# Gathering the attention scores and outputs of a fused attention and gated feed-forward kernel into one block each

## The chip, the cores and the metric

The kernel runs on one core of a Trainium2 chip. The metric is the device time of one execution in microseconds; times are medians of several executions, nearly all of which agree within 0.3%. Almost all executions are with a granted TensorE clock of 0.997 to 1.0 of full speed. The engines are PE (matrix products; PEld is its weight loads), DVE (vector), ACT (activation functions), POOL and SP (here they mostly issue transfers).

## The reference

Four batches of eight heads, 768 positions, head size 64. Each query sees keys less than 16 positions away and one maximum key (with a mean value) for each block of 32 positions; the result is the input of a gated feed-forward layer with a residual:

```python
mask_l = np.abs(pos[:, None] - pos[None, :]) < window          # window 16
scores_all = np.concatenate([scores_l_m, scores_s], axis=-1)   # local, and 24 block keys
a = np.exp(scores_all - max); a = a / (sum + 1e-09)
attn = np.matmul(a, v_all)                                     # v and 24 block means
# ...
g = x @ w_gate; val = x @ w_val                                # x: 3072 x 512, d_ff 1536
ffn_out = gelu(g) * val @ w_out
out = x + sigmoid(x @ w_res) * ffn_out
```

## The kernel before

The work is cut into eight units of 384 positions (half a batch). A unit's feed-forward has a long stage of gate and value products (g and vv, 96 matmuls of 384 columns), then an output stage (f with w_out, r with w_res, 512 columns each). Into the output stage of unit u the attention of unit n = u + 1 is woven, head pair by head pair (four pairs). Its matmuls are small and come in two other forms than the full 128 x 128 ones: a **score** takes 64 rows of the array (one head of the pair in each half), and an **attention output** 64 columns (one tile of 64 queries in each half of the partitions written).

```python
def s_step(u, hp, st, banks=None, tiles=None):      # scores of one pair
    # ... two banks, 384 of 512 columns used in each
    s_mm(u, hp, [x[:, 0:TU] for x in s])            # 12 matmuls
    P = ppool.tile([128, 2, HT, QT], BF16, tag="P", name="P")
    # ... exponential(s) on ACT, one or two instructions
    if u:
        Pf = P.rearrange("p a t q -> p (a t) q")
        nc.vector.tensor_mul(Pf, Pf, maskt.unsqueeze(1).to_broadcast([128, 2 * HT, QT]))

def av_step(u, hp, st, pool=ps_o, tag="ao"):        # outputs of one pair
    # ... 12 matmuls into ao, then
    av_end(hp, st, ao)                              # normalization on DVE

def mid_out(u, st, gvT, nst):                       # output stage of units 1 to 6
    n = u + 1
    other = dict(pool=ps_t, tag="t")
    s_step(n, 0, nst)
    s_step(n, 1, nst, TO2)
    res_step(st, 0)
    res_step(st, 1)
    ffn_step(st, gvT, 0, 0, 4)                      # four of twelve f
    av_step(n, 0, nst)
    xt_dma(0, nst)                                  # transpose for the next unit
    av_step(n, 1, nst, **other)
    xt_dma(1, nst)
    s_step(n, 2, nst)
    s_step(n, 3, nst, MM2)
    # ... (even n: copies on POOL)
    ffn_step(st, gvT, 0, 4, FO)
    ffn_step(st, gvT, 1, 0, 3)
    av_step(n, 2, nst)
    xt_dma(2, nst)
    av_step(n, 3, nst, **other)
    xt_dma(3, nst)
    end_step(u, st, 0)
    ffn_step(st, gvT, 1, 3, FO)
    res_step(st, 2)
    end_step(u, st, 1)
    ffn_step(st, gvT, 2, 0, FO)
    end_step(u, st, 2)
```

Unit 1's attention is woven into unit 0's output stage by another function, `first_out`, which the change leaves as it is.

The softmax here doesn't subtract the row's maximum and nothing guards it: scores larger than these inputs give would overflow.

Of the kernel before, what the change touches and what calls it, by code (L numbers as in the profile page):

```python
# [8 lines left out]
F32 = mybir.dt.float32  # L9
BF16 = mybir.dt.bfloat16  # L10
AF = mybir.ActivationFunctionType
# [4 lines left out]
def kernel(  # L16
# [11 lines left out]
    nc = tc.nc  # L28
    B, H, S, D = q.shape
# [3 lines left out]
    scale = 1.0 / math.sqrt(D)  # L33
# [3 lines left out]
    KO = DM // 128  # L37
    FO = DFF // 128
    QT = 64
    NT = S // QT  # L40
    HT = NT // 2
    TU = S // 2
    NSUB = TU // 128
    NU = 2 * B
    NP = H // 2
# [7 lines left out]
    const = ctx.enter_context(tc.tile_pool(name="const", bufs=1))  # L53
    wpool = ctx.enter_context(tc.tile_pool(name="wpool", bufs=1))
    qk = ctx.enter_context(tc.tile_pool(name="qk", bufs=1))
    work = ctx.enter_context(tc.tile_pool(name="work", bufs=3))
    ppool = ctx.enter_context(tc.tile_pool(name="ppool", bufs=4))
    upool = ctx.enter_context(tc.tile_pool(name="upool", bufs=2))
    ps_mm = ctx.enter_context(tc.tile_pool(name="ps_mm", bufs=4, space=bass.MemoryType.PSUM))
    ps_s = ctx.enter_context(tc.tile_pool(name="ps_s", bufs=1, space=bass.MemoryType.PSUM))  # L60
    ps_o = ctx.enter_context(tc.tile_pool(name="ps_o", bufs=1, space=bass.MemoryType.PSUM))
    ps_t = ctx.enter_context(tc.tile_pool(name="ps_t", bufs=1, space=bass.MemoryType.PSUM))
# [3 lines left out]
    maskt = const.tile([128, QT], BF16, name="maskt")  # L66
# [3 lines left out]
    bias_t = const.tile([128, 1], F32, name="bias_t")  # L70
# [5 lines left out]
    kW = [const.tile([128, NT, NP, 128], BF16, name=f"kW{i}") for i in range(2)]  # L76
    qT = [const.tile([128, NQ, NP, 128], BF16, name=f"qT{i}") for i in range(2)]
    q_nat = const.tile([128, NQ, DM], BF16, name="q_nat")
    vext = [const.tile([128, NT, H, VP], BF16, name=f"vext{i}") for i in range(2)]
    vsum = [const.tile([128, DM], BF16, name=f"vsum{i}") for i in range(2)]  # L80
    vpart = const.tile([128, DM], BF16, name="vpart")
    w_gate = wpool.tile([128, KO, DFF], BF16, name="w_gate")
    w_val = wpool.tile([128, KO, DFF], BF16, name="w_val")
# [55 lines left out]
    with tc.manual_schedule():  # L139
# [159 lines left out]
        def vsum_bc(b, lo, hi, eng):  # L299
            src = vsum[b % 2][96:128, :].rearrange("p (h d) -> p h d", d=D) if b else vblk[96:128, :, 0:D]  # L300
            src = src.unsqueeze(1).to_broadcast([32, hi - lo, H, D])
            eng.tensor_copy(vext[b % 2][96:128, lo:hi, :, 0:D], src)  # L302
# [19 lines left out]
        def s_step(u, hp, st, banks=None, tiles=None):  # L322
            if tiles:
                s, banks = tiles, True
            elif banks:
                s = [p.tile([128, 512], F32, tag=tag, name="s") for p, tag in banks]
            else:
                s2 = ps_s.tile([128, 2, 512], F32, tag="s", name="s")
                s = [s2[:, hh] for hh in range(2)]
            s_mm(u, hp, [x[:, 0:TU] for x in s])  # L330
            P = ppool.tile([128, 2, HT, QT], BF16, tag="P", name="P")
            if banks:
                for hh in range(2):
                    nc.scalar.activation(P[:, hh].rearrange("p t q -> p (t q)"), s[hh][:, 0:TU], AF.Exp,  # L334
                                         scale=scale, bias=bias_t[:])
            else:
                nc.scalar.activation(P.rearrange("p a t q -> p a (t q)"), s2[:, :, 0:TU], AF.Exp,  # L337
                                     scale=scale, bias=bias_t[:])
            if u:
                Pf = P.rearrange("p a t q -> p (a t) q")  # L340
                nc.vector.tensor_mul(Pf, Pf, maskt.unsqueeze(1).to_broadcast([128, 2 * HT, QT]))  # L341
            st["P", hp] = P

        MM2 = ((ps_mm, "mm"),) * 2
        TO2 = ((ps_t, "t"), (ps_o, "ao"))

        def av_step(u, hp, st, pool=ps_o, tag="ao"):
            b, half = u // 2, u % 2
            P = st["P", hp]
            ao = pool.tile([128, NSUB, 2, D + 1], F32, tag=tag, name="ao")  # L350
            for sub in range(NSUB):
                for hh in range(2):
                    for e in range(2):
                        t = 2 * sub + e
                        nc.tensor.matmul(ao[64 * e:64 * e + 64, sub, hh, :], P[:, hh, t, :],  # L355
                                         vext[b % 2][:, half * HT + t, 2 * hp + hh, 0:D + 1],
                                         start=True, stop=True, skip_group_check=True)
            av_end(hp, st, ao)
# [12 lines left out]
        def av_end(hp, st, ao):  # L371
            rz = work.tile([128, NSUB, 2, 1], F32, tag="rz", name="rz")
            nc.vector.reciprocal(rz[:], ao[:, :, :, D:D + 1])  # L373
            xn = st["xn"][:, hp].rearrange("p s (h d) -> p s h d", d=D)
            nc.vector.tensor_mul(xn, ao[:, :, :, 0:D], rz.to_broadcast([128, NSUB, 2, D]))  # L375
# [8 lines left out]
        def xt_dma(ko, st):  # L384
            nc.sync.dma_start_transpose(out=st["xT"][:, ko].rearrange("d (s k) -> d s k", k=128),
                                        in_=st["xn"][:, ko].rearrange("p s d -> p (s d)"))
# [6 lines left out]
        def gv_mm(ps, w, st, fo, kos):  # L393
            for ko in kos:
                nc.tensor.matmul(ps[:, 0:TU], w[:, ko, fo * 128:(fo + 1) * 128], st["xT"][:, ko, :],  # L395
                                 start=(ko == 0), stop=(ko == KO - 1), skip_group_check=True)

        def gv_end(gvT, fo, g, vv):
            ge = work.tile([128, TU], F32, tag="ge", name="ge")
            nc.scalar.activation(ge[:], g[:, 0:TU], AF.Gelu)  # L400
            nc.vector.tensor_mul(gvT[:, fo, :], ge[:], vv[:, 0:TU])  # L401

        def mm_tile(name):
            return ps_mm.tile([128, 512], F32, tag="mm", name=name)
# [13 lines left out]
            gv_end(gvT, 0, g, vv)  # L418

        def fo_last_two(st, gvT):  # L420
            g = [mm_tile("g"), mm_tile("g")]
            for i in range(2):
                gv_mm(g[i], w_gate, st, FO - 2 + i, range(KO))
            for i in range(2):
                vv = mm_tile("vv")
                gv_mm(vv, w_val, st, FO - 2 + i, range(KO))
                gv_end(gvT, FO - 2 + i, g[i], vv)

        def res_step(st, sub):
            ss = slice(sub * 128, (sub + 1) * 128)  # L430
# [7 lines left out]
        def ffn_step(st, gvT, sub, lo, hi):  # L438
            ss = slice(sub * 128, (sub + 1) * 128)
            if lo == 0:  # L440
                st["f", sub] = mm_tile("f")
            for fo in range(lo, hi):
                nc.tensor.matmul(st["f", sub][:], gvT[:, fo, ss], w_out[:, fo, :],  # L443
                                 start=(fo == 0), stop=(fo == FO - 1), skip_group_check=True)
# [32 lines left out]
        mm, t_bank, o_bank = (ps_mm, "mm"), (ps_t, "t"), (ps_o, "ao")  # L477
        keep_warm(12)
        tk, tq, ao = {}, {}, {}
# [11 lines left out]
        st = new_unit()  # L491
        gvT = upool.tile([128, FO, TU], BF16, tag="gvT", name="gvT")
# [66 lines left out]
        s2 = ps_s.tile([128, 2, 512], F32, tag="s", name="gv")  # L559
# [22 lines left out]
        def pool_after(x):  # L582
            nc.gpsimd.tensor_copy(gate2[:], x)
# [31 lines left out]

        def mid_out(u, st, gvT, nst):
            n = u + 1
            other = dict(pool=ps_t, tag="t")
            s_step(n, 0, nst)
            s_step(n, 1, nst, TO2)  # L620
            res_step(st, 0)
            res_step(st, 1)
            ffn_step(st, gvT, 0, 0, 4)
            av_step(n, 0, nst)
            xt_dma(0, nst)
            av_step(n, 1, nst, **other)
            xt_dma(1, nst)
            s_step(n, 2, nst)
            s_step(n, 3, nst, MM2)
            if n % 2 == 0:  # L630
                pool_after(nst["P", 3][0:1, 0, 0, 0:1])
                for i in range(2, 4):
                    vsum_bc(n // 2, 3 * i, 3 * i + 3, nc.gpsimd)
            ffn_step(st, gvT, 0, 4, FO)
            ffn_step(st, gvT, 1, 0, 3)
            av_step(n, 2, nst)
            xt_dma(2, nst)
            av_step(n, 3, nst, **other)
            xt_dma(3, nst)
            end_step(u, st, 0)  # L640
            ffn_step(st, gvT, 1, 3, FO)
            res_step(st, 2)
            end_step(u, st, 1)
            ffn_step(st, gvT, 2, 0, FO)
            end_step(u, st, 2)
# [9 lines left out]
        for u in range(NU):  # L655
            b, half = u // 2, u % 2
# [6 lines left out]
            if u:  # L663
                gvT = upool.tile([128, FO, TU], BF16, tag="gvT", name="gvT")
            for fo in range(0 if u else 2, FO):
# [25 lines left out]
                if half == 1 and nb < B:  # L691
# [11 lines left out]
                    if nb == 1:  # L703
                        if fo == 0:
                            tk = turn_all(k_sb[nb])
                        if fo in (0, 2, 4, 6):
                            hp = (2, 0, 1, 3)[fo // 2]
# [5 lines left out]
            else:  # L713
                nst = new_unit()
                (mid_out if u else first_out)(u, st, gvT, nst)
                st = nst
# [30 lines left out]
```

## Time and profile before

| | before |
|---|---|
| time | 256.43 us (256.35 to 256.56) |
| span of the profile | 254.6 us |
| PE / DVE / ACT busy | 97% / 63% / 51% |
| score matmuls | 384, in the record 9.0 us busy |
| output matmuls in units 1 to 7 | 336, 8.3 us busy |

The two small groups, as the list of PE groups by shape has them (line, shape, count, then busy time and the mean length of one):

```profile
L317 PE MATMUL s<-qT,kW 64*128 64x64 bf16 x384 | 9.0, 191 | 0.0
L355 PE MATMUL ao<-vext,P 128*64 128x65 bf16 x336 | 8.3, 197 | 0.0
```

The second number of a row, 191 ns, is the length of one matmul from start to end, and most of it overlaps its neighbours: 384 x 0.191 would be 73 us, the group holds PE for 9.0. The idle time of both groups is 0.0.

### The profile page before, as it was taken

How to read it: one execution, taken by the hardware profiler on the slowest of the kernel's cores; microseconds unless marked ns; L12 is line 12 of the kernel's file. 1: busy time of each engine (PE TensorE's matmuls, PEld its weight loads, DVE VectorE, ACT ScalarE, POOL GpSimd, SP SyncE). 2: the span in 40 equal slices, each digit the busy share in tenths (PEclk: the TensorE clock that was granted, in tenths of full speed). 3: DMA queues.
4: the chain of work that ended last, by engine and by line, in shares of the span. 5: the costliest groups of instructions: out<-in, count | busy, mean ns of one | idle time of the engine just before them, and what ended most of it. 6: DMA issues, size and time to landing. Idle time of an engine off the chain costs nothing.

```text
span 254.6 us, 5847 instructions
## 1 busy us (share of the span) xinstructions
PE 246.6 (97%) x2303; PEld 139.7 (55%) x2328; DVE 159.4 (63%) x364; ACT 129.6 (51%) x216; POOL 97.3 (38%) x128
## 2 busy tenths in 40 slices
PE   6999999999999999999999999999999999999994
PEld 2676555565545665446544665446545555456544
DVE  6985796397667544858567544958567544854424
ACT  8885468366572337353572337254572337353320
POOL 8895542361506970274406970274404000000000
PEclk9999999999999999999999999999999999999999
DMA  5999999999404999399404999289604400230003
GB/s 80 177 182 197 197 205 207 175 176 222 61 19 121 159 150 150 56 161 171 103 18 120 162 155 153 49 162 170 104 18 115 98 3 0 50 139 0 3 1 124
DMA packets 98107, 29.34 MB, mean 115 GB/s; under 512 B 83224, under 2 KB 94944, under 8 KB 97984
## 3 DMA queue, kind: packets, MB, share of 16 engines
q0 software_dynamic: 68352, 14.76, 66.3%
q1 hardware_dynamic: 29728, 14.21, 25.7%
q8 instruction: 18, 0.29, 0.5%
q14 instruction: 9, 0.07, 0.1%
HBM read 29.36 MB, written 6.29 MB: 140 GB/s over the span
## 4 chain that ended last, share of the span: by engine, by line
PE 93%; DVE 5%; issue 2%; DVEq 0%
PE g L395 25%; PE vv L395 24%; PE f L443 23%; PE r L433 8%; PE s L317 3%; PE ao L355 3%; PE vs L282 1%; PE ao L367 1%; PE tp L220 1%; PE vs L290 1%; DVE ks L237 1%; PE xp L380 1%; DVE o L452 1%; DVE th L449 1%; PE gv L395 1%
## 5 line engine op out<-in xcount | busy, mean ns | idle before, releaser
L401 DVE TENSOR_TENSOR gvT<-ge,vv 128x384 bf16<-128x384 f32 x95 | 52.2, 552 | 48.1 <-PE vv L395 43.9
L400 ACT ACTIVATE ge<-g 128x384 f32<-128x384 f32 x95 | 46.7, 491 | 67.3 <-DVE gvT L401 34.8
L395 PE MATMUL g<-xT,w_gate 128*128 128x384 bf16 x380 | 78.0, 326 | 0.0
L395 PE MATMUL vv<-xT,w_val 128*128 128x384 bf16 x380 | 77.8, 326 | 0.0
L443 PE MATMUL f<-w_out,gvT 128*128 128x512 bf16 x262 | 62.7, 379 | 1.5 <-issue 1.1
L395 PEld LDWEIGHTS <-w_gate 128*128 128x128 bf16 x384 | 37.1, 98 | 26.2 <-issue 1.4
L395 PEld LDWEIGHTS <-w_val 128*128 128x128 bf16 x384 | 37.6, 98 | 24.7
L443 PEld LDWEIGHTS <-gvT 128*128 128x128 bf16 x276 | 25.7, 98 | 29.5
L107 POOL DMA_DIRECT2D vext<-in_v_dram x32 | 24.1, 777 | 15.0 <-DMA w_out<-in_moe_w_out_dram 5.6
L436 ACT ACTIVATE th<-r 128x512 f32<-128x512 f32 x24 | 13.5, 607 | 27.6 <-PE r L433 27.6
L449 DVE SCALAR_TENSOR_TENSOR th<-th,f 128x512 f32<-128x512 f32 (+2 forms) x26 | 16.6, 640 | 14.4 <-PE f L443 14.4
L341 DVE TENSOR_TENSOR P<-P,maskt 128x768 bf16<-128x768 bf16 x28 | 16.2, 580 | 11.0 <-ACT P L337 6.1
L433 PE MATMUL r<-w_res,xT 128*128 128x512 bf16 x88 | 22.7, 380 | 0.4
L302 POOL COPY vext<-vsum 32x1536 bf16<-32x1536 bf16 x12 | 17.2, 1464 | 13.0 <-DMA vsum<-vpart 12.9
L452 DVE SCALAR_TENSOR_TENSOR o<-th,xn 128x512 f32<-128x512 f32 (+2 forms) x26 | 18.2, 701 | 0.9
L375 DVE TENSOR_TENSOR xn<-ao,rz 128x384 bf16<-128x384 f32 x32 | 17.8, 557 | 1.1
L337 ACT ACTIVATE P<-s,bias_t 128x768 bf16<-128x768 f32 x17 | 15.3, 901 | 4.5 <-PE s L317 4.3
L127 POOL DMA_DIRECT2D q_nat<-in_q_dram x18 | 15.8, 899 | 0.9 <-issue 0.7
L334 ACT ACTIVATE P<-s,bias_t 128x384 bf16<-128x384 f32 x30 | 15.7, 579 | 0.0
L237 DVE TENSOR_REDUCE ks<-kW 128x24 bf16<-128x768 bf16 x16 | 15.1, 943 | 0.0
L433 PEld LDWEIGHTS <-xT 128*128 128x128 bf16 x96 | 8.8, 98 | 9.9
L373 DVE RECIPROCAL rz<-ao 128x6 f32<-128x6 f32 x32 | 6.1, 191 | 10.9 <-PE ao L355 10.0
(90 smaller groups left out, 187.1 us busy)
## 6 DMA issues: line engine op xcount, KB each, us to landing
out_dram<-o SPq DMA_DIRECT2D x23, 256.0 KB, 2.2
vext<-in_v_dram POOLq DMA_DIRECT2D x32, 96.0 KB, 6.4
q_nat<-in_q_dram POOLq DMA_DIRECT2D x18, 128.0 KB, 6.4
w_gate<-in_moe_w_gate_dram POOLq DMA_DIRECT2D x6, 256.0 KB, 8.9
w_val<-in_moe_w_val_dram POOLq DMA_DIRECT2D x6, 256.0 KB, 9.3
w_out<-in_moe_w_out_dram POOLq DMA_DIRECT2D x3, 512.0 KB, 14.4
k_nat<-in_k_dram POOLq DMA_DIRECT2D x16, 96.0 KB, 5.8
vext<-vext SPq DMA_DIRECT2D x6, 144.0 KB, 5.4
```

Source lines behind the costliest of these rows:

```text
L107: nc.gpsimd.dma_start(out=vext[b % 2][0:QT, :, h, 0:D], in_=v[b, h].rearrange("(t p) d -> p t d", p=QT))
L237: nc.vector.tensor_reduce(out=ks.rearrange("d (t n) -> d t n", n=2), in_=kw[:, :, 0:QT].rearrange("d t (n w) -> d t n w", w=BLK), axis=myb ...
L302: eng.tensor_copy(vext[b % 2][96:128, lo:hi, :, 0:D], src)
L341: nc.vector.tensor_mul(Pf, Pf, maskt.unsqueeze(1).to_broadcast([128, 2 * HT, QT]))
L375: nc.vector.tensor_mul(xn, ao[:, :, :, 0:D], rz.to_broadcast([128, NSUB, 2, D]))
L395: nc.tensor.matmul(ps[:, 0:TU], w[:, ko, fo * 128:(fo + 1) * 128], st["xT"][:, ko, :], start=(ko == 0), stop=(ko == KO - 1), skip_group_ch ...
L400: nc.scalar.activation(ge[:], g[:, 0:TU], AF.Gelu)
L401: nc.vector.tensor_mul(gvT[:, fo, :], ge[:], vv[:, 0:TU])
L433: nc.tensor.matmul(r[:], st["xT"][:, ko, ss], w_res[:, ko, :], start=(ko == 0), stop=(ko == KO - 1))
L443: nc.tensor.matmul(st["f", sub][:], gvT[:, fo, ss], w_out[:, fo, :], start=(fo == 0), stop=(fo == FO - 1), skip_group_check=True)
L449: nc.vector.scalar_tensor_tensor(th[:, cs], th[:, cs], 1.0, f[:, 0:n], ALU.add, ALU.mult)
L452: nc.vector.scalar_tensor_tensor(o.rearrange("p (k d) -> p k d", d=128), th[:, cs].rearrange("p (k d) -> p k d", d=128), 0.5, x, ALU.mult, ...
```

## The change

The intent: all scores of a unit in one place, in six banks filled to 512 columns, and all outputs in another, with the outputs of the last two pairs computed ahead of their normalizations. Cut to its core:

```diff
-    ppool = ctx.enter_context(tc.tile_pool(name="ppool", bufs=4))
+    p_all = const.tile([128, 2, NP * HT, QT], BF16, name="p_all")
+        def s_all(u):
+            for i in range(3):
+                # i == 0: two banks of the large pool, 1: the double bank, 2: ps_t and ps_o
+                for j in range(8):
+                    hp, t = divmod(8 * i + j, HT)
+                    # ... one score matmul for each of two heads
+                # ... exponentials of 512 columns (i == 1: one of 1024), two masks of 512
+        def av_all(u, st):
+            for hp in range(NP):
+                # ... 12 output matmuls into ps_t, ps_o, and the two halves of the double bank
+                if hp != 2:
+                    for i in range(2 if hp == 3 else hp, hp + 1):
+                        av_end(i, st, aos[i])
+                        if u > 1:
+                            xt_dma(i, st)
 ...
         def mid_out(u, st, gvT, nst):
             n = u + 1
-            other = dict(pool=ps_t, tag="t")
-            s_step(n, 0, nst)
-            s_step(n, 1, nst, TO2)
+            s_all(n)
+            # ... (even n: copies on POOL)
             res_step(st, 0)
             res_step(st, 1)
-            ffn_step(st, gvT, 0, 0, 4)
-            av_step(n, 0, nst)
-            # ... pairs 0 and 1, scores 2 and 3, f, pairs 2 and 3
+            ffn_step(st, gvT, 0, 0, FO)
+            av_all(n, nst)
             end_step(u, st, 0)
-            ffn_step(st, gvT, 1, 3, FO)
+            ffn_step(st, gvT, 1, 0, FO)
```

In `fo_last_two` the Gelus of the last two gate products are also written ahead of the value products.

More of the change, by code (lines that the diff above doesn't have):

```diff
@@ L330, in s_step @@
             s_mm(u, hp, [x[:, 0:TU] for x in s])
-            P = ppool.tile([128, 2, HT, QT], BF16, tag="P", name="P")
+            P = p_all[:, :, hp * HT:(hp + 1) * HT]
             if banks:
@@ L339, in s_step @@
             if u:
-                Pf = P.rearrange("p a t q -> p (a t) q")
-                nc.vector.tensor_mul(Pf, Pf, maskt.unsqueeze(1).to_broadcast([128, 2 * HT, QT]))
+                nc.vector.tensor_mul(P, P, maskt.unsqueeze(1).unsqueeze(1).to_broadcast([128, 2, HT, QT]))
             st["P", hp] = P
+        def s_all(u):
+            b, half = u // 2, u % 2
+            kw, qt = kW[b % 2], qT[b % 2]
+            s2 = None
+            for i in range(3):
+                if i == 0:
+                    s = [ps_mm.tile([128, 512], F32, tag="mm", name="s") for _ in range(2)]
+                elif i == 1:
+                    s2 = ps_s.tile([128, 2, 512], F32, tag="s", name="s")
+                    s = [s2[:, hh] for hh in range(2)]
+                else:
+                    s = [p.tile([128, 512], F32, tag=tag, name="s") for p, tag in TO2]
+                for j in range(8):
+                    hp, t = divmod(8 * i + j, HT)
+                    tt = half * HT + t
+                    for hh in range(2):
+                        ps = slice(hh * 64, hh * 64 + 64)
+                        nc.tensor.matmul(s[hh][:, j * QT:(j + 1) * QT], kw[ps, tt, hp, :],
+                                         qt[ps, tt // 2, hp, (tt % 2) * QT:(tt % 2 + 1) * QT],
+                                         start=True, stop=True, skip_group_check=True)
+                js = slice(8 * i, 8 * i + 8)
+                m = maskt.unsqueeze(1).to_broadcast([128, 8, QT])
+                for hh in range(1 if i == 1 else 2):
+                    if i == 1:
+                        nc.scalar.activation(p_all[:, :, js].rearrange("p a j q -> p a (j q)"), s2[:], AF.Exp,
+                                             scale=scale, bias=bias_t[:])
+                    else:
+                        nc.scalar.activation(p_all[:, hh, js].rearrange("p j q -> p (j q)"), s[hh][:], AF.Exp,
+                                             scale=scale, bias=bias_t[:])
+                for hh in range(2):
+                    nc.vector.tensor_mul(p_all[:, hh, js], p_all[:, hh, js], m)
@@ new lines, in av_all @@
+        def av_all(u, st):
+            b, half = u // 2, u % 2
+            aos = []
+            for hp in range(NP):
+                if hp < 2:
+                    pool, tag = TO2[hp]
+                    ao = pool.tile([128, NSUB, 2, D + 1], F32, tag=tag, name="ao")
+                else:
+                    if hp == 2:
+                        s2 = ps_s.tile([128, 2, 512], F32, tag="s", name="ao")
+                    ao = s2[:, hp - 2, 0:NSUB * 2 * (D + 1)].rearrange("p (s h d) -> p s h d", s=NSUB, h=2)
+                for sub in range(NSUB):
+                    for hh in range(2):
+                        for e in range(2):
+                            t = 2 * sub + e
+                            nc.tensor.matmul(ao[64 * e:64 * e + 64, sub, hh, :], p_all[:, hh, hp * HT + t, :],
+                                             vext[b % 2][:, half * HT + t, 2 * hp + hh, 0:D + 1],
+                                             start=True, stop=True, skip_group_check=True)
+                aos.append(ao)
+                if hp != 2:
[3 more added lines that the diff above has]
+                            xt_dma(i, st)
@@ L420, in fo_last_two @@
         def fo_last_two(st, gvT):
-            g = [mm_tile("g"), mm_tile("g")]
+            ge = []
             for i in range(2):
-                gv_mm(g[i], w_gate, st, FO - 2 + i, range(KO))
+                g = mm_tile("g")
+                gv_mm(g, w_gate, st, FO - 2 + i, range(KO))
+                ge.append(work.tile([128, TU], F32, tag="ge", name="ge"))
+                nc.scalar.activation(ge[i][:], g[:, 0:TU], AF.Gelu)
             for i in range(2):
@@ L426, in fo_last_two @@
                 gv_mm(vv, w_val, st, FO - 2 + i, range(KO))
-                gv_end(gvT, FO - 2 + i, g[i], vv)
+                nc.vector.tensor_mul(gvT[:, FO - 2 + i, :], ge[i][:], vv[:, 0:TU])
         def res_step(st, sub):
@@ L617, in mid_out @@
             n = u + 1
-            other = dict(pool=ps_t, tag="t")
-            s_step(n, 0, nst)
-            s_step(n, 1, nst, TO2)
+            s_all(n)
+            if n % 2 == 0:
+                pool_after(p_all[0:1, 1, 4 * HT - 1, 0:1])
+                for i in range(2, 4):
+                    vsum_bc(n // 2, 3 * i, 3 * i + 3, nc.gpsimd)
             res_step(st, 0)
             res_step(st, 1)
-            ffn_step(st, gvT, 0, 0, 4)
-            av_step(n, 0, nst)
-            xt_dma(0, nst)
-            av_step(n, 1, nst, **other)
-            xt_dma(1, nst)
-            s_step(n, 2, nst)
-            s_step(n, 3, nst, MM2)
-            if n % 2 == 0:
-                pool_after(nst["P", 3][0:1, 0, 0, 0:1])
-                for i in range(2, 4):
-                    vsum_bc(n // 2, 3 * i, 3 * i + 3, nc.gpsimd)
-            ffn_step(st, gvT, 0, 4, FO)
-            ffn_step(st, gvT, 1, 0, 3)
-            av_step(n, 2, nst)
-            xt_dma(2, nst)
-            av_step(n, 3, nst, **other)
-            xt_dma(3, nst)
+            ffn_step(st, gvT, 0, 0, FO)
+            av_all(n, nst)
             end_step(u, st, 0)
-            ffn_step(st, gvT, 1, 3, FO)
+            ffn_step(st, gvT, 1, 0, FO)
             res_step(st, 2)
```

## The prediction

> **What bounds the kernel now.** I read the page first (busy shares, then the chain that ended last), then the PE groups by shape, then the timeline of one output stage, then the lists of waits.
>
> ```profile
> PE 246.6 (97%) x2303; PEld 139.7 (55%) x2328; DVE 159.4 (63%) x364; ACT 129.6 (51%) x216; POOL 97.3 (38%) x128
> ...
> PE 93%; DVE 5%; issue 2%; DVEq 0%
> PE g L395 25%; PE vv L395 24%; PE f L443 23%; PE r L433 8%; PE s L317 3%; PE ao L355 3%; PE vs L282 1%; PE ao L367 1%; PE tp L220 1%; PE vs L290 1%; DVE ks L237 1%; PE xp L380 1%; DVE o L452 1%; DVE th L449 1%; PE gv L395 1%
> ```
>
> The matmul engine is the bound: 97% busy, and 93% of the chain that ended last is PE. Of its 254.6 us span the score matmuls (s) hold 3% and the attention outputs (ao, two lines) 4%; the large products that the change doesn't touch hold the rest. So the change can only win in how PE passes between these, or lose by making PE wait. Busy time can't show a pass, since the ends of matmuls are modelled; start times can. Here is the output stage of unit 2 (it computes unit 3's attention), cut to what I use; columns are start, length, engine, line, operation, count, and idle time before with its releaser:
>
> ```profile
> 96.59 1.46 PE L395 MATMUL vv<-xT,w_val 128*128 128x384 bf16 x8
> ...
> 97.30 1.28 ACT L337 ACT_TABLE_LOAD   x1
> 97.51 1.21 DVE L401 TENSOR_TENSOR gvT<-ge,vv 128x384 bf16<-128x384 f32 x2 [1.40 <-PE vv L395]
> 97.98 0.41 PEld L317 LDWEIGHTS <-kW 64*128 64x128 bf16 x24 [0.32 <-issue]
> ...
> 98.44 1.41 PEld L433 LDWEIGHTS <-xT 128*128 128x128 bf16 x8
> ...
> 99.39 1.05 ACT L334 ACTIVATE P<-s,bias_t 128x384 bf16<-128x384 f32 x2
> 99.53 0.56 DVE L341 TENSOR_TENSOR P<-P,maskt 128x768 bf16<-128x768 bf16 x1 [0.81 <-ACT P L337]
> ...
> 100.18 1.03 PE L443 MATMUL f<-w_out,gvT 128*128 128x512 bf16 x4
> ...
> 101.13 0.46 PEld L355 LDWEIGHTS <-P 128*64 128x64 bf16 x24 [0.42 <-DVE P L341]
> 101.63 0.41 PEld L317 LDWEIGHTS <-kW 64*128 64x128 bf16 x24
> 102.09 2.06 PEld L443 LDWEIGHTS <-gvT 128*128 128x128 bf16 x11
> 102.50 5.80 SPq L385 DMA_TRANSPOSE xT<-xn  x4
> ...
> 104.57 0.46 PEld L355 LDWEIGHTS <-P 128*64 128x64 bf16 x24 [0.42 <-DVE P L341]
> 105.07 1.62 PEld L443 LDWEIGHTS <-gvT 128*128 128x128 bf16 x9
> 107.03 1.03 PE L433 MATMUL r<-w_res,xT 128*128 128x512 bf16 x4
> 109.53 0.18 POOL L583 COPY gate<-xT 1x1 bf16<-1x1 bf16 x1 [4.34 <-DMA xT<-xn]
> 110.48 0.65 PE L395 MATMUL g<-xT,w_gate 128*128 128x384 bf16 x3
> ```
>
> The reader should see four blocks of small matmuls (97.98, 101.13, 101.63, 104.57) between runs of full ones. A full 512-column matmul starts every 0.217 us (eight r plus four f from 98.44 to 101.04); 24 scores take 98.44 - 97.98 = 0.46 us, 24 outputs 101.63 - 101.13 = 0.50. From the first score to the next g at 110.48 the stage is 12.50 us: 48 scores 0.92, 48 outputs 1.00, 36 f and 12 r 10.40, together 12.32. Left over is 0.18.
>
> That 0.18 sits ahead of the two blocks of outputs. Four f from 100.18 would free PE at 101.05, the outputs start at 101.13; eleven f from 102.09 would end at 104.48, the outputs start at 104.57. The step from the gate/value products into the scores costs the same: the last vv starts at 97.73, would be followed at 97.89, the first score starts at 97.98. The brackets call the weight load before the outputs a wait for the masks on DVE, but in unit 3's stage the mask ended 0.10 us before the outputs, and the gap after the last f is the same, so it is the switch. Passes from small blocks to full ones, and from outputs to scores, cost nothing visible.
>
> **What the Trainium skill says.** "TensorEngine Tiling (Array Packing)", section Key Properties: changing the tiling mode drains TensorE. The trace agrees in one direction: about 0.09 us on entering a small block from full matmuls, none measurable on leaving. "TensorE: Matmul & The Clock Gate", section Back-to-back issue gap: an isolated warm gap of N/2.4 + 2.5 ns, 216 ns for 512 columns; the trace has 217. "ScalarE: Activation LUTs", section What ACT_TABLE_LOAD costs: 1283 ns for the load of a table; the trace has 1283 for each of the seven loads ahead of the exponentials, which is why no exponential starts before 98.59. "VectorE: DVE Perf Modes", section on the 8-slice pipeline in each mode: packed 16-bit operands give two results a cycle. The trace agrees: a mask over 768 bf16 elements takes 580 ns, a product of 384 f32 elements 552.
>
> **The change, part by part.** It concerns six stages (the attention of units 2 to 7). I count from the stage's first score, T = 0.
>
> *Switches.* Before, PE enters a small block from full matmuls three times (scores, outputs, outputs); after, twice. One entry of 0.09 us less in each of six stages: 0.55 us. No matmul is removed: 48 scores and 48 outputs stay.
>
> *Exponentials.* Before, two of 768 columns and four of 384; after, four of 512 and one of 1024. From 901 and 579 ns, 0.84 ns a column; the 384-column ones start 0.53 us apart and the 768-column one is followed 0.80 us later, so 512 columns take 0.63 and 1024 about 1.02. Sum 4 x 0.63 + 1.02 = 3.55 against 2 x 0.80 + 4 x 0.53 = 3.7: 0.15 less, off the path. They begin when the table is loaded (T = 0.61), end about T = 4.2.
>
> *Masks.* Before, four of 580 ns; after, six of 512 columns, 580 - 256 x 0.52 = 447 ns each: 2.7 against 2.3 us. The last one follows the last exponential, T = 4.75.
>
> *When PE needs them.* Scores T = 0 to 0.92, eight r and twelve f to 0.92 + 20 x 0.217 = 5.26, a switch, outputs from 5.35 to 6.35. The first needs only the masks of the first group; the last pair, at 6.1, needs the mask of T = 4.75. No wait, 1.3 us to spare. The scores' banks are free in time too: the two packed banks in the large pool were the last two gate products', read by the Gelus before the table load at 97.30.
>
> *Normalizations and transposes.* The four now come together. Before, the outputs' start at 101.13 leads to the first transpose's issue at 102.50, 1.37 later; after, T = 6.72. DVE then needs 0.75 us a pair (191 + 557 ns), but the four transposes leave their queue 1.28 us apart (102.50 and 103.78 before), so the issues are 6.72, 8.0, 9.28 and 10.56. Landing takes 2.3 us: the fourth arrives at T = 12.9. The next unit's first three parts start at T = 12.41 and its fourth part is asked for six matmuls of 0.1625 us later, T = 13.38. So 0.5 us to spare, where before it was 109.4 against 111.46, 2.0 us. This is the tightest place.
>
> *Sum.* 256.43 - 0.55 = 255.9. The change of the Gelus ahead of the value products and the buffer of P move no instruction on the path; each pair's P was already held once per unit (four buffers, four pairs).
>
> **The rivals.** (1) *A wait for the last transpose replaces the switch.* For: 0.5 us to spare, while single transposes landed in up to 3.7 us, and the queue would carry four in a row. Against: in the three stages that gate a load on it, the fourth landed 2.3 to 2.5 us after issue. If it came 0.8 late throughout, 0.3 us a stage, 6 x 0.3 = 1.8: 257.7.
> (2) *The query load comes too late.* POOL holds the next queries' load until the fourth transpose has landed, now 1.3 us later (T = 12.9 against 11.55). In units 3 and 5 the transposed queries landed at 125.2 and 182.7, the scores started at 127.04 and about 184.85: slack 1.8 and 2.1. What remains is 0.5 to 0.9; a loss of a microsecond in two stages would give 257 to 258.
> (3) *All P in one tensor ties engines together.* If the build orders accesses by the range that they span, the 1024-column exponential, which spans both heads, waits for the masks of the first group: 0.5 us later, masks end at 5.3, still before T = 6.1. Only if each group waited for all masks of the one before would the masks end near T = 7.2, PE stop for 1 to 2 us a stage, and the time be 262 to 268. The before kernel works in slices of shared tensors throughout and shows no such waits; I give it 3%.
> (4) *The bound moves to DVE or ACT.* DVE is at 8.3 us of this stage's 12.5, ACT at 7.2; 0.4 more and 0.15 less change nothing.
>
> **Range and chances.** Certain is only the one switch per stage; a switch hidden in the passes that I see as free could add as much again (255.3). Against it stand small waits of rivals 1 and 2. I say 255.9 us, 255.1 to 257.6. 2% is 5.1 us: a gain of that is nine times what the switches hold (1%); a loss of that needs rival 3 or a stall of 0.9 us in every stage (4%).
>
> **What would show it.** Right: in the changed profile the outputs of all four pairs start about 5.35 us after the first score, in one block of 48; from first score to next g about 12.4 us; the fourth transpose lands before the fourth part of g asks for it; no new PE wait in the list. Wrong: a gap in g before its fourth part (rival 1), scores late behind a query transpose in two stages (rival 2), exponentials with idle time ahead of them released by masks (rival 3), or a pace of scores other than 0.019 us or of outputs other than 0.021 us in the longer blocks.

## The result, and the profile after

| | before | changed |
|---|---|---|
| time, median | 256.5 us (256.35 to 256.77, 4 runs) | 254.5 us (254.38 to 255.01, 4 runs) |
| ratio | 1 | 0.9925, 95% interval 0.9907 to 0.9942 |
| span of the profile | 254.6 us | 252.9 us |
| first score to next g, unit 2 | 12.50 us | 12.17 us |

Ratios here are the mean time of one kernel's fast runs over that of the other's in the same rounds, so not quite the ratio of the medians. Executions over 1.5% slower than the fastest of the same kernel are left out of the means. The change gained 2.0 us where 0.55 was predicted, and 254.5 lies below the range of 255.1 to 257.6. It is still "within 2%", which had been given 95%.

The page of the changed kernel, its line of PE and its chain:

```profile
PE 248.1 (98%) x2328; PEld 139.5 (55%) x2328; DVE 159.0 (63%) x376; ACT 127.9 (51%) x210; POOL 96.5 (38%) x128
...
PE g L451 25%; PE vv L451 24%; PE f L502 24%; PE r L492 8%; PE ao L390 2%; PE s L360 2%; PE vs L282 1%; PE tp L220 1%; PE ao L423 1%; PE vs L290 1%; PE s L317 1%; PE wp L534 1%; DVE ks L237 1%; DVE o L511 1%; PE xp L436 1%
```

The bound is the same. PE's busy time even rises, from 246.6 to 248.1 us, while the kernel gets faster; the page before had 2303 matmul records and this one 2328, all of them, so here the difference is one of missing records. The chain alone shows no cause. Start times do. The same stage as in the prediction, the changed kernel, PE only (start, length, engine, line, operation, count):

```profile
97.67 0.87 PE L360 MATMUL s<-qT,kW 64*128 64x64 bf16 x48
98.48 1.90 PE L492 MATMUL r<-w_res,xT 128*128 128x512 bf16 x8
100.22 2.75 PE L502 MATMUL f<-w_out,gvT 128*128 128x512 bf16 x12
102.90 0.95 PE L390 MATMUL ao<-vext,p_all 128*64 128x65 bf16 x48
103.78 2.76 PE L502 MATMUL f<-w_out,gvT 128*128 128x512 bf16 x12
106.39 1.03 PE L492 MATMUL r<-w_res,xT 128*128 128x512 bf16 x4
107.25 2.75 PE L502 MATMUL f<-w_out,gvT 128*128 128x512 bf16 x12
109.84 0.65 PE L451 MATMUL g<-xT,w_gate 128*128 128x384 bf16 x3
```

The 48 scores hold PE for 98.48 - 97.67 = 0.81 us. Before, two blocks of 24 took 0.46 each, 0.92 together. The 48 outputs hold it for 103.78 - 102.90 = 0.88 us, before 0.50 and 0.50. So the blocks themselves became 0.23 us shorter though no matmul is missing. With the one entry less (0.09 to 0.10) that is the stage's 0.33 us, and six stages of it are the 2.0 us. All six have it: from first score to next g they take 12.16 to 12.17 us in the changed kernel, and 12.49 to 12.50 before (12.62 in one).

**The theory** that this suggests ("passes"): PE pays about 0.11 us at every pass from one form of matmul to another, in either direction and between the two small forms too. The start times of single matmuls agree. In the changed kernel the scores start in pairs 29 ns apart, the last pair at 98.355 and 98.358, and the first r at 98.480: 0.12 us after, not 0.03. In the kernel before, the last output of the first block starts at 101.510 and the next score at 101.637, 0.13 us after. Counted this way, a stage had seven passes: full to scores, scores to full, full to outputs, outputs to scores, scores to full, full to outputs, outputs to full. The change leaves four. Three times 0.11 is 0.33.

**The rivals:** "packing" (scores are cheaper because they fill six banks and need fewer, larger exponentials), "waits" (something that PE waited for, masks or banks, went away), and "the Gelus" (the small edit in `fo_last_two`).

### The profile page after: what moved, and what is told of

Same layout as the page of the kernel before. It is cut to its first block, busy times and chain, and to the rows that moved or that the text cites. A ratio compares the mean times of both kernels' runs of the same rounds, so it can differ in the third digit from the quotient of the medians.

```text
span 252.9 us, 5881 instructions
## 1 busy us (share of the span) xinstructions
PE 248.1 (98%) x2328; PEld 139.5 (55%) x2328; DVE 159.0 (63%) x376; ACT 127.9 (51%) x210; POOL 96.5 (38%) x128
## 4 chain that ended last, share of the span: by engine, by line
PE 93%; DVE 5%; issue 1%; DVEq 0%
PE g L451 25%; PE vv L451 24%; PE f L502 24%; PE r L492 8%; PE ao L390 2%; PE s L360 2%; PE vs L282 1%; PE tp L220 1%; PE ao L423 1%; PE vs L290 1%; PE s L317 1%; PE wp L534 1%; DVE ks L237 1%; DVE o L511 1%; PE xp L436 1%
## 5 line engine op out<-in xcount | busy, mean ns | idle before, releaser
L456 ACT ACTIVATE ge<-g 128x384 f32<-128x384 f32 x81 | 39.7, 490 | 61.0 <-DVE gvT L457 30.0
L502 PE MATMUL f<-w_out,gvT 128*128 128x512 bf16 x276 | 63.6, 379 | 0.0
L373 DVE TENSOR_TENSOR p_all<-p_all,maskt 128x512 bf16<-128x512 bf16 x36 | 14.2, 423 | 8.3 <-ACT p_all L370 4.5
L511 DVE SCALAR_TENSOR_TENSOR o<-th,xn 128x512 f32<-128x512 f32 (+2 forms) x26 | 16.9, 651 | 0.9
L370 ACT ACTIVATE p_all<-s,bias_t 128x512 bf16<-128x512 f32 x24 | 15.2, 692 | 0.1
```

The lines of the kernel that those rows point to most:

```text
L456: nc.scalar.activation(ge[:], g[:, 0:TU], AF.Gelu)
L502: nc.tensor.matmul(st["f", sub][:], gvT[:, fo, ss], w_out[:, fo, :], start=(fo == 0), stop=(fo == FO - 1), skip_group_check=True)
L511: nc.vector.scalar_tensor_tensor(o.rearrange("p (k d) -> p k d", d=128), th[:, cs].rearrange("p (k d) -> p k d", d=128), 0.5, x, ALU.mult, ...
```

## The experiments

Thirteen runs, all correct. The first four alter the changed kernel without touching packing: three add passes, the fourth only moves them.

**Scores in two blocks.** The first r is put between the 32 scores of the first two groups and the 16 of the third:

```diff
-            s_all(n)
+            s_all(n, (0, 1))
+            res_step(st, 0)
+            s_all(n, (2,))
             # ... (even n: copies on POOL)
-            res_step(st, 0)
             res_step(st, 1)
```

> Changed kernel, with its 48 scores cut in 32 and 16 by the four matmuls of the first r; banks, exponentials and masks as in the changed kernel. Theory 'passes' (every pass of PE from one form of matmul to another costs about 0.11 us, also on leaving a small block, so the change saved three passes of seven in a stage): two passes more, 6 x 0.22 = 1.3 us, so 254.5 + 1.3 = 255.8, and the two blocks of scores last about 0.58 and 0.35 us, 0.12 more in sum than the one block of 0.81. Rival 'packing' (scores are cheaper because they fill six banks, with fewer and larger exponentials): nothing of that is undone, so at most the entry of 0.09 us, 255.0 or less. Rival 'waits' (the gain was waits for masks and banks that went): 254.5 to 255.0.

Measured: 256.1 us (255.79 to 256.23), ratio to the kernel before 0.9977 (0.9965 to 0.999): 0.3 above what passes gave, 1.1 above the most that its rivals allowed. The timeline of unit 2's stage:

```profile
97.95 0.64 PE L360 MATMUL s<-qT,kW 64*128 64x64 bf16 x32
98.52 1.04 PE L492 MATMUL r<-w_res,xT 128*128 128x512 bf16 x4
99.49 0.41 PE L360 MATMUL s<-qT,kW 64*128 64x64 bf16 x16
99.83 1.04 PE L492 MATMUL r<-w_res,xT 128*128 128x512 bf16 x4
...
110.32 0.65 PE L451 MATMUL g<-xT,w_gate 128*128 128x384 bf16 x3
```

Thirty-two scores take 0.57 us, sixteen 0.34. With 0.46 for 24 and 0.81 for 48, the four lengths lie on one line: about 0.105 us for the block and 14.7 ns for each matmul (from 16 and 48: 0.47 / 32 = 0.0147; 0.34 - 16 x 0.0147 = 0.105). The stage is 12.37 us, 0.20 more than the changed kernel's.

**Scores in three blocks.** The same, with both r products between the three groups.

```diff
-            s_all(n)
+            s_all(n, (0,))
+            res_step(st, 0)
+            s_all(n, (1,))
+            res_step(st, 1)
+            s_all(n, (2,))
             # ... (even n: copies on POOL)
-            res_step(st, 0)
-            res_step(st, 1)
```

> Changed kernel, with its 48 scores cut in three blocks of 16 by the two r products. Passes: four passes more per stage, 6 x 0.44 = 2.6 us, 257.1, slower than the kernel before although all packing stays. Packing or waits: two entries of 0.09, at most 6 x 0.18 = 1.1, 255.6.

Measured: 257.0 us (256.89 to 257.35), ratio 1.0019 (1.0006 to 1.0031). All of the change's packing is in this kernel, and it is slower than the kernel before. That rules out packing as the cause, and waits too, for which at most 255.6 had been expected; the list of PE's waits has only that of the first matmul, 1.2 us. The stage is 110.69 - 98.10 = 12.59 us, 0.42 more than the changed kernel's for four passes more.

```profile
98.10 0.41 PE L360 MATMUL s<-qT,kW 64*128 64x64 bf16 x16
98.44 1.04 PE L492 MATMUL r<-w_res,xT 128*128 128x512 bf16 x4
99.41 0.41 PE L360 MATMUL s<-qT,kW 64*128 64x64 bf16 x16
...
110.69 0.65 PE L451 MATMUL g<-xT,w_gate 128*128 128x384 bf16 x3
```

**Outputs in two blocks.** Pairs 0 and 1 after eight f, pairs 2 and 3 after all twelve.

```diff
-            ffn_step(st, gvT, 0, 0, FO)
-            av_all(n, nst)
+            ffn_step(st, gvT, 0, 0, 8)
+            av_all(n, nst, (0, 1), aos)
+            ffn_step(st, gvT, 0, 8, FO)
+            av_all(n, nst, (2, 3), aos)
```

> Changed kernel, with the outputs of pairs 0 and 1 after eight f and those of pairs 2 and 3 after all twelve. Passes: two more per stage, 1.3 us, less up to 0.4 because the first transposes leave 0.9 us earlier and the fourth part of g need not wait (0.18, 0.08 and 0.18 us in the profile of the changed kernel): 255.4 to 255.8. Rivals: 254.1 to 254.6.

Measured: 255.86 us (255.83 to 255.91), ratio 0.9971 (0.9959 to 0.9983). That is 0.06 above what passes gave and 1.3 above the most that the rivals allowed. The two blocks of 24 are back at 0.50 us each. So the outputs' form pays as the scores' does.

**Outputs earlier.** In the first profile of the changed kernel the next unit's fourth part of g started 0.18, 0.08 and 0.18 us late in three stages (units 5, 6 and 7): rival 1 of the prediction, in small. The first of them, with the three parts that precede it:

```profile
166.42 0.65 PE L451 MATMUL g<-xT,w_gate 128*128 128x384 bf16 x3
166.91 0.65 PE L451 MATMUL vv<-xT,w_val 128*128 128x384 bf16 x3
167.57 0.32 PE L451 MATMUL g<-xT,w_gate 128*128 128x384 bf16 x1
```

Six matmuls of 0.1625 us from 166.42 would have led to 167.395. This run moves the outputs ahead by four f, the passes being the same:

```diff
-            ffn_step(st, gvT, 0, 0, FO)
-            av_all(n, nst)
+            ffn_step(st, gvT, 0, 0, 8)
+            av_all(n, nst)
+            ffn_step(st, gvT, 0, 8, FO)
```

> Changed kernel, with all 48 outputs after eight f in place of twelve: same four passes. If the late fourth transpose costs what the profile shows (0.44 us in three stages together), 254.5 - 0.4 = 254.1 and no gap before the fourth part of g; if the last masks (4.5 us after the first score) come too late for the last pair's outputs (at 4.9), a wait of up to 0.3 us a stage takes it back, 254.5 or more.

Measured: 254.46 us (254.28 to 254.56), ratio 0.9915 (0.9902 to 0.9928). The gaps are gone from its profile, but the time is that of the changed kernel. The profiled execution of the changed kernel was the one of 255.01 us; its other three took 254.38 to 254.50. So the late fourth part costs little in most executions. The unaltered changed kernel fits that:

> The changed kernel once more, for a second profile and more times beside the next three: 254.5. If the waits of the fourth part of g (0.44 us in the first profile) come only in some executions, a profile of 252.4 to 252.6 us has none.

Measured: 254.61 us (254.43 to 254.92), ratio 0.9923 (0.9911 to 0.9935). Its profile, of 252.5 us, still has one such gap, of 0.1 us in one stage, so not quite none.

**The cost of a pass, by itself.** Four kernels start from the kernel before and put extra small matmuls between g and vv in nine of the twelve steps of units 2 to 7, 54 places in all. Their operands are zeros and their results are thrown away; only their form differs.

```diff
             gv_mm(g, w_gate, st, fo, range(KO))
+            if extra:
+                x = ps_s.tile([128, 2, 512], F32, tag="s", name="x")
+                for hh in range(2):                       # rows: ps is one half of the partitions
+                    nc.tensor.matmul(x[:, hh, 0:64], warm[ps, 0:128], warm[ps, 128:192], ...)
+                # columns: matmul(x[ps, 0, 0:64], warm[:, 0:64], warm[:, 128:192], ...)
+                # full:    matmul(x[:, hh, 0:64], warm[:, 0:128], warm[:, 128:192], ...)
             vv = mm_tile("vv")
```

> Kernel before, with two extra matmuls of 64 columns between g and v in nine of the twelve steps of units 2 to 7 (54 places), in the form of their neighbours (128 rows, 128 columns of weights), results thrown away. Both theories: no change of form, so only their own time, 0.05 to 0.15 us a place, 2.7 to 8 us: 259 to 264.5.

> The same 54 places, the two extra matmuls in the scores' form (64 rows, one for each half). Passes: entry 0.09, the pair 0.03, leaving 0.12, so 0.24 us a place, 13 us: 269.5. If only entering costs (as the prediction had it): 0.09 + 2 x 0.019 = 0.13, 7 us: 263.5.

> The same 54 places, the two extra matmuls in the outputs' form (64 columns of weights, one for each half of the partitions written). Passes: 0.09 + 0.03 + 0.13 = 0.25 us a place, 13.5 us: 270. If only entering costs: 0.09 + 2 x 0.021, 7 us: 263.5.

> Kernel before, in the 54 places a pair in the scores' form and right after it a pair in the outputs' form. If a pass between the two small forms costs what leaving for full ones costs: entry 0.09, pair, 0.12, pair, 0.13, about 0.37 us a place, 20 us: 276.5. If it is free, as the prediction had it: 0.27, 14.5 us: 271. If it costs as much as leaving and entering: 0.48, 26 us: 282.5.

| extra at each of 54 places | time (median) | more than the median of before | per place |
|---|---|---|---|
| two full matmuls of 64 columns | 259.65 us | 3.17 us | 0.059 us |
| a pair in the scores' form | 269.32 us | 12.84 us | 0.238 us |
| a pair in the outputs' form | 270.18 us | 13.70 us | 0.254 us |
| one pair of each, in a row | 277.83 us | 21.13 us | 0.391 us |

(The kernel before took 256.48 us in the call of the first three and 256.70 in that of the fourth.) A pair in a block takes 0.029 us. Taking that off and dividing by the passes: (0.238 - 0.029) / 2 = 0.105, (0.254 - 0.029) / 2 = 0.113, (0.391 - 2 x 0.029) / 3 = 0.111 us a pass. A pair of each in a row has three passes and not four, and the measured time follows that count: the pass between the two small forms costs as much as one to or from the full form. One place, from the timeline of the kernel with a pair of each:

```profile
90.50 0.81 PE L395 MATMUL g<-xT,w_gate 128*128 128x384 bf16 x4
91.24 0.20 PE L413 MATMUL x<-warm 64*128 64x64 bf16 x2
91.38 0.22 PE L417 MATMUL x<-warm 128*64 128x64 bf16 x2
91.53 0.82 PE L395 MATMUL vv<-xT,w_val 128*128 128x384 bf16 x4
```

Four g from 90.50 would free PE at 91.15. The first pair starts 0.09 later, the second 0.14 after it, vv 0.15 after that. The same place with two full matmuls, which start when the g are through and hand over after 0.06:

```profile
91.69 0.81 PE L395 MATMUL g<-xT,w_gate 128*128 128x384 bf16 x4
92.34 0.22 PE L412 MATMUL x<-warm 128*128 128x64 bf16 x2
92.40 0.81 PE L395 MATMUL vv<-xT,w_val 128*128 128x384 bf16 x4
```

One more rival lies near: a load of weights takes 0.098 us in the profile, about as much as a pass, and a short matmul could be too short to hide it. The two full matmuls load weights just as often, and the whole pair costs 0.059 us. The start times of the loads (PEld) show where the pass lies. Within a run of full matmuls a load starts well ahead of its matmul: in the kernel before, the loads of the four r behind f start at 106.81 and these r at 107.03. Behind the scores, the loads of r and r itself both start at 98.44. At each of the 54 places with a pair of each form, all three passes have the first load of the new form 1 to 5 ns ahead of its matmul. So at a pass nothing is loaded ahead, and the 0.1 us lies before the load, not in it.

**The Gelus alone**, in the kernel before:

```diff
-            g = [mm_tile("g"), mm_tile("g")]
-            # ... both gate products; then for each: value product, Gelu, product on DVE
+            # ... for each: gate product, Gelu; then for each: value product, product on DVE
```

> Kernel before with one part of the change alone, the last two Gelus written ahead of the value products. All theories: the engine orders stay, 256.4 +- 0.3. If it gains more than 0.5 us, part of the change's gain is this.

Measured: 256.43 us (256.26 to 256.79), ratio 0.9986 (0.9948 to 1.0024; one run of the kernel before took 259.83 us, at a clock of 0.986, and widens the interval). The median is that of the kernel before: this part does nothing measurable.

**The same in the stage that the change left alone.** Unit 1's attention, woven into unit 0's output stage, has ten passes. Gathering it should save six, 0.66 us. The first try:

```diff
         def first_out(u, st, gvT, nst):
-            # ... scores 0 and 1, r, 4 f, outputs 0 and 1, scores 2, f in thirds by row, ...
+            s_all(n)
+            # ... two r
+            ffn_step(st, gvT, 0, 0, 8)
+            av_all(n, nst)
+            ffn_step(st, gvT, 0, 8, FO)
+            # ... the rest row by row
```

> Changed kernel with the outputs after eight f, and unit 1's attention (the one stage that the change left alone) gathered in the same way. That stage then has four passes in place of ten: passes predicts 6 x 0.11 = 0.66 us, 253.8. Rival packing: the same gain per unit as in the others, 0.33, so 254.1. If the four transposes on PE at the end of that stage wait for their copies, less.

Measured: 255.21 us (255.17 to 257.14), ratio 0.9955 (0.9932 to 0.9978), slower than the changed kernel. A miss, and its timeline says why (the bracket is idle time and what ended it):

```profile
42.17 1.02 PE L502 MATMUL f<-w_out,gvT 128*128 128x512 bf16 x4 [0.47 <-DMA w_out<-in_moe_w_out_dram]
43.13 0.95 PE L390 MATMUL ao<-vext,p_all 128*64 128x65 bf16 x48
44.82 2.32 PE L502 MATMUL f<-w_out,gvT 128*128 128x512 bf16 x9 [0.74 <-DMA w_out<-in_moe_w_out_dram]
```

In this stage w_out is still arriving in three parts. The old order used the first part for all three rows of tiles, then the second, then the third, which hid the transfer; working row by row asks for the second and third part earlier and waits for both, 1.2 us by the brackets. They count from a modelled end of the matmul before; by start times PE lost 1.4 us (42.17 where 41.54 was due, 44.82 where 44.01 was), which is the whole distance to the 253.8 us expected. On top of this kernel, a further try put the block sums of v right behind the outputs to save one more pass in two units:

```diff
             av_all(n, nst)
+            if u in (2, 4):
+                vsum_grp(n // 2 + 1, ps_mm, "mm")
```

> As earlier_and_first, and in two units the twelve small matmuls of the block sums of v stand right behind the outputs, in place of a spot of their own among the g and v products. One pass less in each of two stages, 0.22 us: 253.6. If v has not landed by then, PE waits and it is slower.

Measured: 256.56 us (255.56 to 261.66), ratio 0.999 (0.9969 to 1.0011), worse and scattered; the 261.66 is the slow execution, and the five fast ones took 255.56 to 257.36 (median 256.28). The profile, of the fastest, shows the same waits for w_out and three small delays that the run before does not have, 0.55 us together: the first block sums start 0.13 us later behind the outputs than in the other unit, and two vv start 0.12 and 0.30 us late (119.97 and 176.74), each 0.05 us after a product on DVE ended. That is more than the 0.22 us of two passes. What slowed the other executions is not settled.

The mended version uses w_out in the order in which it lands:

```diff
             s_all(n)
             # ... three r
+            ffn_step(st, gvT, 0, 0, 8)
+            av_all(n, nst)
+            ffn_step(st, gvT, 1, 0, 8)
+            # ... transposes of pairs 0 and 1
+            ffn_step(st, gvT, 2, 0, 8)
+            # ... transposes of pairs 2 and 3
+            for sub in range(NSUB):
+                ffn_step(st, gvT, sub, 8, FO)
+                end_step(u, st, sub)
```

> As earlier_and_first, but the products f of unit 0 use w_out in the order in which its three parts land (parts one and two for all three rows first, the third last). Account by passes: the waits for w_out go, the stage has four passes in place of ten, 254.5 - 0.66 = 253.8. If the account fails in this stage: 254.4 or more without any wait for w_out in the list.

Measured: 253.79 us (253.78 to 253.84), ratio to the kernel before 0.9893 (0.9877 to 0.991). This beats both kernels. The list of PE's waits has no w_out any more, and the timeline of the stage shows the blocks:

```profile
38.28 0.87 PE L360 MATMUL s<-qT,kW 64*128 64x64 bf16 x48
39.09 2.76 PE L492 MATMUL r<-w_res,xT 128*128 128x512 bf16 x11
41.69 1.89 PE L502 MATMUL f<-w_out,gvT 128*128 128x512 bf16 x8
43.51 0.95 PE L390 MATMUL ao<-vext,p_all 128*64 128x65 bf16 x48
44.39 1.90 PE L502 MATMUL f<-w_out,gvT 128*128 128x512 bf16 x7
...
51.12 0.81 PE L451 MATMUL g<-xT,w_gate 128*128 128x384 bf16 x4
```

First score to next g is 51.12 - 38.28 = 12.84 us. In the kernel before this stage ran from 38.15 to 51.65, 13.50 us. The 0.66 between them is six passes of 0.11.

## Why the prediction was wrong

The step that failed is one sentence of the section on what bounds the kernel: "Passes from small blocks to full ones, and from outputs to scores, cost nothing visible." It was reached by taking the whole length of a block, 0.46 us for 24 scores and 0.50 for 24 outputs, as its matmuls' own time, and carrying it over as a pace of 0.019 and 0.021 us each. The sum of the stage then closed with only 0.18 us left over, and that seemed to leave room for the two entries and nothing else. The closing sum proved nothing, because the cost of leaving was already inside the block lengths. Blocks of 16, 24, 32 and 48 show it: a fixed 0.105 us and 14.7 ns each. The prediction named this as a way to be wrong ("a pace of scores other than 0.019 us or of outputs other than 0.021 us in the longer blocks") and had 255.3 for a switch hidden in the passes, but allowed for one hidden switch per stage, where there were two.

Point by point:

- *The bound, and that no PE wait would take the place of what was removed*: right. PE is the bound after as before; the only PE wait listed in the changed kernel's profile is that of its first matmul, 1.2 us at the start.
- *Switches, 0.55 us*: the entry of 0.09 us was right, and one entry fewer per stage. The term was mis-sized because two departures fewer per stage, 0.11 from the scores and 0.12 from the outputs, were priced at nothing. With them, 6 x 0.33 = 2.0 us, which is what was measured.
- *Exponentials and masks*: right and off the path. In the changed profile the exponentials ran from 0.61 to 4.03 us after the first score (4.2 predicted), the masks took 423 ns each (447 predicted) and ended at 4.49 (4.75 predicted), the outputs started at 5.23.
- *Rival 1, the last transpose*: the slack was even smaller than the 0.5 us forecast. In unit 2's stage POOL saw the fourth transpose landed at 110.80 and the matmul that needs it started at 110.81, as early as the six parts before it allow (109.84 + 6 x 0.1625); in three later stages it was 0.08 to 0.18 late, in one execution. It cost little in the median. (In the kernel before, four stages gate a load on the fourth transpose, not three.)
- *Rival 2, the queries*: did not come to pass, but only just. The scores of unit 4 started at 126.40, which is 0.10 after the last vv made room (eight from 125.00), the ordinary entry; their queries had landed at 126.36, so 0.04 us was left where 0.5 to 0.9 was forecast. Unit 6 had 0.31 us (182.84 against 183.15), and in the second profile of the changed kernel it was 0.93 and 0.64. The forecast had misread one start: "about 184.85" is where r begins (184.87); the scores begin at 184.41, so that slack was 1.7 us, not 2.1. *Rival 3, exponentials held up by masks*: no such wait; they follow each other without idle time. *Rival 4*: DVE and ACT stay at 63% and 51%.
- *The Gelus and the one tensor for P move nothing*: right for the Gelus by their own run. The tensor alone was not tried; its only possible harm, waits, is absent.

Why the hardware charges a pass is not shown by these runs. They show that the charge depends on the form changing, not on the size, that it is near the same for the three kinds of pass tried, and that the first weights of the new form are not loaded until it is over.

## What to carry to other kernels

Where PE is the bound and matmuls of different array forms alternate, count the passes between forms: here each cost 0.11 us whichever way it went, about as much as seven small matmuls, so blocks of one form want to be long and few. Never take the length of a block divided by its count as the price of one matmul; compare two block lengths, so that a fixed part shows. When work is gathered into longer blocks, check what the old order was hiding: here it was a weight matrix still on its way, and keeping to its order of arrival turned a loss of 0.7 us into a gain of as much.

## What the Trainium skill lacked or had wrong

- "TensorEngine Tiling (Array Packing)", Key Properties, says that changing the mode drains TensorE, but gives no cost and doesn't say that it is paid in each direction and between two tiled modes. Here: 0.105 to 0.113 us a pass, from 54 inserted pairs and from blocks of four lengths.
- "TensorE: Matmul & The Clock Gate", Back-to-back issue gap, gives about 131 ns a matmul for a sustained stream of weight load and 512-column matmul. The trace has 217 ns in the streams read here (twelve f in 2.60 us), which is the page's figure for an isolated gap.
- "ScalarE: Activation LUTs", What ACT_TABLE_LOAD costs, adds about 1380 ns of drain to the 1283 ns of a load. In unit 2's stage of the changed kernel the load follows the last Gelu by 0.02 us (96.97 to 96.99) and the first exponential starts 0.01 us after it (98.28); only the 1.28 us are to be seen.
